# Linear attention and two feed-forward networks on one core: seven products reordered, one accumulation delayed, decode ticks and two attention steps changed

## Chip, core and metric

The kernel runs on one core of a Trainium2 chip. The metric is the device time of one execution in microseconds (us). The core's engines are TensorE (PE, with its weight loads listed as PEld), VectorE (DVE), ScalarE (ACT), GpSimd (POOL) and SyncE (SP), which here only issues transfers. Each engine works through its own queue in order.

## What is computed

Linear attention over 8 batches of 8 heads (576 positions of 64), then a feed-forward network with squared ReLU (512 to 2048 to 512) and a gated one with a norm ahead of it (512 to 1536 to 512), for 4608 tokens, all in float32.

```python
q_s = softmax(q, axis=-1);  k_s = softmax(k, axis=2)      # both with the maximum taken off first
kv = einsum('bhsd,bhse->bhde', k_s, v)
x = einsum('bhsd,bhde->bhse', q_s, kv)                    # heads joined: (4608, 512)
h = relu(x @ w_in);  x = (h * h) @ w_out                  # first network
xn = x / sqrt(mean(x * x) + 1e-6) * rms_g                 # second network
g = xn @ w_gate
out = (g * sigmoid(g) * (xn @ w_val)) @ w_out2
```

## The kernel before

**Precision.** TensorE multiplies in a rounded format. Each float32 operand is split into a high half (ScalarE copies it into that format) and a low half (VectorE or GpSimd subtracts); `split` (L76) does this for activations. A product takes three passes (`PASSES`, L21): high by high, high by low, low by high, in this order. Only the third needs the low half of the activations when these are the first operand, as in the accumulations.

**First network.** Nine blocks of 512 tokens run one after the other, with 16 units each (`units`, L823). A unit c first makes its hidden slice (`p1_A`, L593: 12 matmuls into a `ps_h` bank, of which there are two; then ReLU at L589, square at L590 and the split of `g` at L77 and L78). Its second-layer product (`p1_B`, L608: 12 matmuls into four `acc` banks) follows `LAG` = 2 units later: the list `pending` (L906 to L908) holds the units that wait for it. After unit 15 the four banks are copied to `e` tiles, two by ScalarE (L622) and two by VectorE (L620), and stored; the next block's first accumulation into a bank waits for its copy. Below, h(n) and o(n) are the first- and second-layer products of the n-th unit over all blocks, so h(32) opens the third block.

**Beside it.** The attention of the next block runs between the units at fixed offsets (`A_STEPS`, `todo`): the maximum of k over positions (`a_kmax`, L402), its transposes (`ps_kt`, `ps_kb`), exponentials, k times v (`ps_kv`, `kvf`, `kvd`), the transposes of q (`ps_q`, `qT`) and `ps_x`, which becomes the next block's input. `a_qn` (L490) divides q by its row sums, on GpSimd. In the first block all attention steps come at the start, in an order written out at L880.

**Decode.** The weights arrive as 64-bit floats. `tick` (L325) moves a job through load, word steps (GpSimd L216, ScalarE L224), three VectorE steps (L235, L243, L247), and the split (ScalarE L251, GpSimd L252), and the halves go back to memory, to be streamed later through a ring of seven `ws` tiles. `n_ticks` (L825) says how many ticks have been made by unit i: the first network's weights in the first block, the second's (36 jobs with 512 values per partition, in groups of six) from the third block on, one tick in two units. The recording layer sorts instructions by readiness and this program order, so where a step stands in its engine's queue is not only set by the tick; steps marked `held` keep their place.

**Second network.** Again nine blocks. Each has six groups n. A group makes two pairs of hidden slices by seven products of half size instead of eight (`STEPS`, L707; p2_A, L724): sums of the weight quarters (a11, s2, a12, s1, s3, s4, a22) times sums of the input quarters (b11, t2, ...), 12 matmuls each, into the banks x, y, v and w. x takes a11 and a12, y takes s2 and s3, v takes s1 and s4. Between two products that share a bank, the first one's value is read out: `p1` (L769), `u2` (L771), `p5` (L776). The second-layer accumulations `p2_B` (L795) of the group before stand after the third and the fifth product. The weights stream in the order `order2` (L118 to L126), of which 16 keys are kept resident. `B_TASKS` (L843) make the next block's input meanwhile: load, squares (`sq`, L637, in `e` tiles, whose four buffers the output copies use too), norm, and the sums and splits of the input quarters.

Of the kernel before, what the change touches and what calls it, by code (L numbers as in the profile page):

```python
# [8 lines left out]
F32 = mybir.dt.float32  # L9
# [5 lines left out]
ALU = mybir.AluOpType  # L15
AX = mybir.AxisListType
# [8 lines left out]
def attention_moe_kernel(  # L25
# [12 lines left out]
    nc = tc.nc  # L38
    B, H, S, D = q.shape
    NT, DM = out.shape  # L40
    P = 128
# [5 lines left out]
    FF1 = w_in.shape[0]  # L47
# [67 lines left out]

    PROD = ("a11", "s2", "a12", "s1", "s3", "s4", "a22")  # L118
    order2 = []
    for n in range(NQ):  # L120
        order2 += [(w, n) for w in PROD[:3]]
# [280 lines left out]
    def a_kmax(j, hp):  # L402
        if j >= B:
            return
        mk = pools["a"].tile([P, 2, D], F32, tag="mk", name="mk", bufs=2)
        kt = kts[j, hp]
        m2 = pools["a"].tile([P, 2, 2, D], F32, tag="m2", name="m2", bufs=1)
        nc.vector.tensor_max(out=m2, in0=kt[:, :, 0:2, :], in1=kt[:, :, 2:4, :])
        nc.vector.tensor_max(out=mk, in0=m2[:, :, 0], in1=m2[:, :, 1])
        nc.vector.tensor_max(out=mk[0:SR], in0=mk[0:SR], in1=kt[0:SR, :, SF, :])  # L410
        mks[j, hp] = mk

# [77 lines left out]
    def a_qn(j, hp):  # L490
        qt = qts.pop((j, hp))
        rs = qms.pop((j, hp)).rearrange("p (h c) -> p h c", h=2).unsqueeze(3)
        qn = pools["a"].tile([P, NG, 2, D], F32, tag="qn", name="qn", bufs=2)
        ins = nc.gpsimd.tensor_tensor(
            out=qn.rearrange("p c h d -> p h c d"),
            in0=qt,
            in1=rs.to_broadcast([P, 2, NG, D]),
            op=ALU.mult,
        )
        held(j, ins)  # L500
        qns[j, hp] = qn
# [198 lines left out]
    def b_x(j, n):  # L700
# [6 lines left out]
    STEPS = (  # L707
        ("a11", "b11", "x"),
        ("s2", "t2", "y"),
        ("a12", "b21", "x"),  # L710
        ("s1", "t1", "v"),
        ("s3", "t3", "y"),
        ("s4", "b22", "v"),
        ("a22", "t4", "w"),
# [9 lines left out]
    def p2_A(j, n, step):  # L724
        a, b, bank = STEPS[step]
        w, x = wt[a, n], xos[j, b]
        if bank not in ps2:
            pool, tag = (ps_h, "h") if bank in "xy" else (ps_a, "a")
            ps2[bank] = pool.tile([P, 512], F32, tag=tag, name=f"ps_{bank}")
            first = True  # L730
        else:
            first = False
        ps = ps2[bank]
        last = bank == "w" or not first
        for g in range(2):
            for kk in range(2):
                for m, (wa, xa) in enumerate(PASSES):
                    nc.tensor.matmul(  # L738
                        ps[:, g * HF : (g + 1) * HF],
                        w[:, wa, (2 * g + kk) * P : (2 * g + kk + 1) * P],  # L740
                        x[:, xa, kk, :],
                        start=first and g == 0 and kk == 0 and m == 0,
                        stop=last and kk == 1 and m == 2,
                        skip_group_check=True,
                    )
        used((a, n), j)

        def sv(name):
            sv2[name] = pools["x"].tile([P, 512], F32, tag=name, name=name, bufs=1)
            return sv2[name]  # L750

        def add(name, in0, in1):
            nc.vector.tensor_tensor(out=sv(name), in0=in0, in1=in1, op=ALU.add)  # L753

        def r_tile(c):
            r = gp.tile([P, T], F32, tag="r", name="r", bufs=2)
            rs[c] = r
            return r

        def done(c):  # L760
            g = gp.tile([P, 2, T], F32R, tag="g", name="g")
            split(g, rs.pop(c))
            ghl[2, j, c] = g

        def two(t):
            return t.rearrange("p (one g f) -> p one g f", one=1, g=2)

        if step == 0:
            nc.scalar.activation(out=sv("p1"), in_=ps, func=AF.Copy)  # L769
        elif step == 1:  # L770
            add("u2", ps, sv2["p1"])  # L771
        elif step == 2:
            r = r_tile(2 * n)
            gate(1, two(ps2.pop("x")), r[:, 0:HF].unsqueeze(1))
        elif step == 3:
            nc.scalar.activation(out=sv("p5"), in_=ps, func=AF.Copy)  # L776
        elif step == 4:
            add("u3", ps2.pop("y"), sv2["p1"])
        elif step == 5:
            add("c12", ps2.pop("v"), sv2["u2"])  # L780
            gate(1, two(sv2["c12"]), rs[2 * n][:, HF:T].unsqueeze(1))
            done(2 * n)
        else:
            c2 = pools["x"].tile([P, 2, 2, HF], F32, tag="c2", name="c2", bufs=1)
            for t, in0, in1 in ((1, sv2["p5"], sv2["u3"]), (0, ps2.pop("w"), sv2["u3"])):
                nc.vector.tensor_tensor(
                    out=c2[:, t].rearrange("p g f -> p (g f)"), in0=in0, in1=in1, op=ALU.add
                )
            r = r_tile(2 * n + 1)
            gate(2, c2, r.rearrange("p (t f) -> p t f", t=2))  # L790
            done(2 * n + 1)
# [33 lines left out]
    def n_ticks(i):  # L825
        if i < FF1:
            return min(NJ1 + 3, 4 + sum(d <= i for d in due.values()))
        return min(NJ1 + 4 + max(0, i - 2 * FF1 - 1) // 2, len(jobs) + 4)


    A_STEPS = ((-3, a_loadk), (-2, a_loadq), (0, a_qmax), (0, a_kmax), (1, a_qsub), (1, a_ktr))
# [17 lines left out]
    with ExitStack() as ctx_a:  # L849
# [44 lines left out]
        for i, (j, c) in enumerate(units):  # L894
            if i == AHEAD:
                ctx_s.close()
                pools["r"] = ctx_r.enter_context(
                    tc.tile_pool(name="rp", bufs=1, reuse_waits="tile")
                )
            if i == 2 * FF1:  # L900
                ctx_r.close()
                pools["q"] = ctx_q.enter_context(
                    tc.tile_pool(name="qp", bufs=1, reuse_waits="tile")
                )
            p1_A(j, c)
            pending.append((j, c, None))  # L906
            if len(pending) > LAG:
                p1_B(*pending.pop(0)[:2])  # L908
            while ticks[0] < n_ticks(i):
                tick()  # L910
            if i > 2 * FF1 and outs:
                outs.pop(0)()
            if ticks[0] > NJ1 + 4:
                flush()
            for n, ja, hp, f in todo.get(i, ()):
                f(ja, hp)
            if i == n1 - FF1 - 1:
                assert not outs and ticks[0] == len(jobs) + 4
                flush(all=True)
                ctx_q.close()  # L920
                ctx_a.close()
                pools["x"] = ctx.enter_context(
                    tc.tile_pool(name="bp", bufs=1, reuse_waits="tile")
                )
                for key in res2[:NX]:
                    place(key)
            s = (i - (n1 - FF1)) * 3 - 6
            for at, f, args in B_TASKS:
                if s <= at < s + 3:
                    f(0, *args)  # L930
# [62 lines left out]
```

## Time and profile before

| | us |
|---|---|
| median of three runs (lowest, highest) | 1847.7 (1846.8, 1851.98) |
| the profiled execution's own time | 1849.58 |
| its span, first to last instruction | 1847.8 |
| TensorE busy in the span (share) | 1761.0 (95%) |
| VectorE busy | 1050.1 (57%) |
| ScalarE busy | 752.9 (41%) |
| GpSimd busy | 358.1 (19%) |
| mean granted TensorE clock | 0.981 |

A row of the timeline has start, duration, engine, line, operation, tiles (out<-in) and, in brackets, how long the engine stood before it and what ended that. [...] The first network's blocks end near 970 us, the second's fill the rest.

### The profile page before, as it was taken

What the parts mean: (1) busy time and instruction counts of PE and PEld (TensorE: products, weight loads), DVE (VectorE), ACT (ScalarE), POOL (GpSimd) and SP (SyncE); (2) the same over time, 40 slices, a digit from 0 to 9 for tenths busy, and PEclk for the clock granted to TensorE, in tenths of its full rate; (3) what the DMA queues carried; (4) which work ended last, traced back from release to release, by engine and by line L of the source; (5) the groups of instructions that cost most, each with busy time, mean ns of one, the idle gap of its engine ahead of it and who ended that gap; (6) DMA issues with size and microseconds to landing.
All of it is one profiled execution on the core that took longest, in us unless ns stands there. A gap on an engine that the chain in (4) does not pass through costs nothing.

```text
span 1847.8 us, 27313 instructions
## 1 busy us (share of the span) xinstructions
PE 1761.0 (95%) x10346; PEld 1526.1 (83%) x10346; DVE 1050.1 (57%) x1820; ACT 752.9 (41%) x1371; POOL 358.1 (19%) x353
## 2 busy tenths in 40 slices
PE   5789997998999899999999999999999999999998
PEld 3568886876887688788888989999999999998997
DVE  7876467366436633422245756576767675757544
ACT  4455444454445544443444232333333333333322
POOL 4666226145326612220000000000000000000000
PEclk8799998999999999999999999999999999999999
DMA  6677657578769866565757766767676767676673
GB/s 173 215 258 268 211 188 247 181 266 284 254 189 323 272 190 200 191 234 182 289 193 241 227 240 213 252 209 258 209 260 209 257 208 258 207 251 217 218 230 124
DMA packets 173634, 420.19 MB, mean 227 GB/s; under 512 B 57408, under 2 KB 74816, under 8 KB 172352
## 3 DMA queue, kind: packets, MB, share of 16 engines
q1 hardware_dynamic: 162272, 377.55, 62.6%
q10 hardware_dynamic: 11232, 40.90, 5.7%
q8 instruction: 83, 1.36, 0.3%
q14 instruction: 47, 0.39, 0.1%
HBM read 358.62 MB, written 59.77 MB: 226 GB/s over the span
## 4 chain that ended last, share of the span: by engine, by line
PE 68%; DMA 8%; DVE 3%; ACT 2%; POOL 1%; issue 1%; SPq 0%; POOLq 0%; ACTq 0%; DVEq 0%
PE acc L98 27%; PE ps_h L98 12%; PE ps_x L738 8%; PE ps_y L738 8%; PE ps_v L738 8%; PE ps_w L738 4%; DMA wd_a<-so 2%; DMA out<-e 2%; DMA wd_s<-so 2%; DMA qt<-in_q 1%; DMA wd_u<-so 1%; PE ps_x L98 1%; PE ps_kv L526 1%; DVE t L243 1%; DVE t L235 1%
## 5 line engine op out<-in xcount | busy, mean ns | idle before, releaser
L78 DVE TENSOR_TENSOR g<-r,g 128x512 fp32r<-128x512 f32 x252 | 191.2, 759 | 266.7 <-ACT g L77 264.5
L98 PE MATMUL acc<-g,ws 128*128 128x512 f32 x1296 | 317.0, 393 | 19.1 <-DVE e L620 8.1
L98 PE MATMUL ps_h<-x,ws 128*128 128x512 f32 x1296 | 329.5, 404 | 5.7 <-POOL ws L252 3.8
L98 PEld LDWEIGHTS acc<-g,ws 128*128 128x128 f32 x1296 | 243.9, 189 | 73.8 <-POOL ws L252 8.6
L98 PEld LDWEIGHTS ps_h<-x,ws 128*128 128x128 f32 x1296 | 245.2, 194 | 58.5 <-POOL ws L252 5.2
L98 PE MATMUL acc<-ws,g 128*128 128x512 f32 x1080 | 268.7, 394 | 0.0
L98 PEld LDWEIGHTS acc<-ws,g 128*128 128x128 f32 x1080 | 196.8, 190 | 36.8
L77 ACT ACTIVATE g<-r 128x512 fp32r<-128x512 f32 x252 | 157.6, 626 | 44.7 <-DVE r L722 30.9
L589 ACT ACTIVATE r<-ps_h 128x512 f32<-128x512 f32 x144 | 85.4, 593 | 194.8 <-PE ps_h L98 194.5
L720 ACT ACTIVATE sg<-c 128x256 f32<-128x256 f32 x108 | 56.5, 524 | 263.3 <-DVE c L753 213.3
L753 DVE TENSOR_TENSOR u<-ps_y,p 128x512 f32<-128x512 f32 x108 | 73.7, 682 | 125.9 <-PE ps_y L738 125.9
L738 PE MATMUL ps_x<-x,ws 128*128 128x256 f32 x972 | 130.7, 284 | 9.8 <-ACT p L769 9.8
L738 PEld LDWEIGHTS ps_x<-x,ws 128*128 128x128 f32 x972 | 122.2, 192 | 11.5 <-ACT p L769 11.4
L738 PEld LDWEIGHTS ps_v<-x,ws 128*128 128x128 f32 x864 | 114.2, 191 | 6.3
L738 PE MATMUL ps_v<-x,ws 128*128 128x256 f32 x864 | 116.0, 282 | 0.0
L98 PE MATMUL ps_h<-x,w 128*128 128x512 f32 x432 | 108.9, 399 | 0.0
L98 PE MATMUL acc<-g,w 128*128 128x512 f32 x432 | 106.9, 396 | 1.8 <-POOL w L252 1.4
L776 ACT ACTIVATE p<-ps_v 128x512 f32<-128x512 f32 x54 | 32.3, 597 | 176.5 <-PE ps_v L738 176.5
L738 PE MATMUL ps_y<-x,ws 128*128 128x256 f32 x756 | 101.0, 283 | 0.0
L98 PEld LDWEIGHTS acc<-g,w 128*128 128x128 f32 x432 | 82.3, 192 | 19.7 <-POOL w L252 1.9
L738 PEld LDWEIGHTS ps_y<-x,ws 128*128 128x128 f32 x756 | 95.7, 192 | 0.7
L98 PEld LDWEIGHTS ps_h<-x,w 128*128 128x128 f32 x432 | 80.0, 190 | 17.8 <-DVE x L78 0.5
(114 smaller groups left out, 2517.6 us busy)
## 6 DMA issues: line engine op xcount, KB each, us to landing
ws<-wd_s SPq DMA_DIRECT2D x135, 512.0 KB, 4.3
ws<-wd_a SPq DMA_DIRECT2D x117, 512.0 KB, 4.5
ws<-wd_o SPq DMA_DIRECT2D x96, 512.0 KB, 4.2
ws<-wd_i SPq DMA_DIRECT2D x90, 512.0 KB, 4.2
ws<-wd_u SPq DMA_DIRECT2D x90, 512.0 KB, 4.2
raw<-in_w_out SPq DMA_DIRECT2D x28, 512.0 KB, 4.8
raw<-in_w_gv SPq DMA_DIRECT2D x24, 512.0 KB, 5.2
wd_s<-so ACTq DMA_DIRECT2D x24, 512.0 KB, 5.4
```

Of the source, the lines that this page charges most:

```text
L77: held(j, nc.scalar.activation(out=dst[:, 0], in_=src, func=AF.Copy))
L78: nc.vector.tensor_tensor(out=dst[:, 1], in0=src, in1=dst[:, 0].bitcast(F32), op=ALU.subtract)
L98: ins = nc.tensor.matmul(ps, lhsT(a), rhs(b), start=first and n == 0, stop=last and n == 2)
L235: nc.vector.tensor_scalar(out=t, in0=sb, scalar1=3, scalar2=0x7FFFFFFF, op0=ALU.logical_shift_left, op1=ALU.bitwise_and,)
L243: nc.vector.scalar_tensor_tensor(out=t, in0=sb, scalar=0x80000000, in1=t, op0=ALU.bitwise_and, op1=ALU.bitwise_or)
L526: ins = nc.tensor.matmul(ps[h * D : (h + 1) * D, 0 : D + 1], ke[0:m, c, h, :], vt[0:m, c, h, :], start=c == 0, stop=c == SF,)
L589: nc.scalar.activation(out=r, in_=ps, func=AF.Relu)
L720: nc.scalar.activation(out=r, in_=h[:, :, 0], func=AF.Sigmoid)
L738: nc.tensor.matmul(ps[:, g * HF : (g + 1) * HF], w[:, wa, (2 * g + kk) * P : (2 * g + kk + 1) * P], x[:, xa, kk, :], start=first and g == ...
L753: nc.vector.tensor_tensor(out=sv(name), in0=in0, in1=in1, op=ALU.add)
L776: nc.scalar.activation(out=sv("p5"), in_=ps, func=AF.Copy)
```

## The change

Five edits, in the order of the file:

- **Order of products.** s1 becomes the third of the seven, a12 the fourth, in `STEPS` and in the order in which the weights stream (`PROD`). The gate of bank x moves behind a12, the copy `p5` behind s1. The accumulations still stand after the third and the fifth product.
- **Maximum of k.** Two pairwise maxima over the four position groups become one reduction along a strided view.
- **q in the first block** is normalized on VectorE instead of GpSimd.
- **Ticks.** From the third block on, ticks are made only in units 2 to 12 of a block, seven in ten units.
- **Block starts of the first network.** At unit 2 of every block but the first no second-layer product is issued; at unit 3 two are.

```diff
-    PROD = ("a11", "s2", "a12", "s1", "s3", "s4", "a22")
+    PROD = ("a11", "s2", "s1", "a12", "s3", "s4", "a22")
...
-        m2 = pools["a"].tile([P, 2, 2, D], F32, tag="m2", name="m2", bufs=1)
-        nc.vector.tensor_max(out=m2, in0=kt[:, :, 0:2, :], in1=kt[:, :, 2:4, :])
-        nc.vector.tensor_max(out=mk, in0=m2[:, :, 0], in1=m2[:, :, 1])
+        nc.vector.tensor_reduce(
+            out=mk, in_=kt[:, :, 0:SF].rearrange("p h c d -> p h d c"), axis=AX.X, op=ALU.max
+        )
...
-        ins = nc.gpsimd.tensor_tensor(
+        ins = (nc.gpsimd if j > 0 else nc.vector).tensor_tensor(
...
         ("s2", "t2", "y"),
+        ("s1", "t1", "v"),
         ("a12", "b21", "x"),
-        ("s1", "t1", "v"),
...
-        return min(NJ1 + 4 + max(0, i - 2 * FF1 - 1) // 2, len(jobs) + 4)
+        at = [n for n in range(2 * FF1 + 1, i + 1) if 2 <= n % FF1 <= 12]
+        return min(NJ1 + 4 + len(at) * 7 // 10, len(jobs) + 4)
...
-            if len(pending) > LAG:
+
+            while len(pending) > (LAG + 1 if j > 0 and c == LAG else LAG):
                 p1_B(*pending.pop(0)[:2])
```

The order on TensorE in the second network, first block, second group of products. `ps_x` is a11, then a12; `ps_y` s2, then s3; `ps_v` s1; the `acc` rows are the accumulation of the block's first hidden slice. Before:

```order
L738 MATMUL ps_x<-x,ws 128x256 x12
L738 MATMUL ps_y<-x,w_8235 128x256 x12
L738 MATMUL ps_x<-x,ws 128x256 x12
L98 MATMUL acc_9111<-ws,g 128x512 x3
L98 MATMUL acc_9112<-ws,g 128x512 x3
L98 MATMUL acc_9113<-ws,g 128x512 x3
L98 MATMUL acc_9114<-ws,g 128x512 x3
L738 MATMUL ps_v<-x,w_8237 128x256 x12
L738 MATMUL ps_y<-x,ws 128x256 x12
```

The same place on TensorE with the change:

```order
L738 MATMUL ps_x<-x,ws 128x256 x12
L738 MATMUL ps_y<-x,w_8171 128x256 x12
L738 MATMUL ps_v<-x,ws 128x256 x12
L98 MATMUL acc_9045<-ws,g 128x512 x3
L98 MATMUL acc_9046<-ws,g 128x512 x3
L98 MATMUL acc_9047<-ws,g 128x512 x3
L98 MATMUL acc_9048<-ws,g 128x512 x3
L738 MATMUL ps_x<-x,w_8173 128x256 x12
L738 MATMUL ps_y<-x,ws 128x256 x12
```

s1 and a12 have changed places around the accumulation, and the resident weight (`w_`, not `ws`) is another one.

The order on TensorE at the start of the third block in the first network. The first `ps_h` row is h(34), the `acc` rows are o(32), the block's first accumulation. Before:

```order
L98 MATMUL ps_h<-x,ws 128x512 x12
L98 MATMUL acc_2744<-g,ws 128x512 x3
L98 MATMUL acc_2745<-g,ws 128x512 x3
L98 MATMUL acc_2746<-g,ws 128x512 x3
L98 MATMUL acc_2747<-g,ws 128x512 x3
L419 MATMUL ps_kt<-ident,mk 128x128
L98 MATMUL ps_h<-x,ws 128x512 x12
```

The same place on TensorE with the change:

```order
L98 MATMUL ps_h<-x,ws 128x512 x12
L419 MATMUL ps_kt<-ident,mk 128x128
L98 MATMUL ps_h<-x,ws 128x512 x12
L98 MATMUL acc_2752<-g,ws 128x512 x3
L98 MATMUL acc_2753<-g,ws 128x512 x3
L98 MATMUL acc_2754<-g,ws 128x512 x3
L98 MATMUL acc_2755<-g,ws 128x512 x3
```

h(35) and a transpose of k now stand ahead of o(32).

The order on VectorE at the same block start, from the split of g(32) on; L620 are the copies of the second and the fourth bank, L235, L243 and L247 the decode. Before:

```order
L78 TENSOR_TENSOR g<-r,g 128x512
L235 TENSOR_SCALAR t_3646<-s 128x512
L243 SCALAR_TENSOR_TENSOR t_3646<-s,t_3646 128x512
L247 ISA t_3646<-t_3646,n 128x1024
L235 TENSOR_SCALAR t_3770<-s 128x512
L243 SCALAR_TENSOR_TENSOR t_3770<-s,t_3770 128x512
L235 TENSOR_SCALAR t_3909<-s 128x512
L247 ISA t_3770<-t_3770,n 128x1024
L620 COPY e<-acc_2089 128x512
L243 SCALAR_TENSOR_TENSOR t_3909<-s,t_3909 128x512
L620 COPY e<-acc_2091 128x512
L485 TENSOR_REDUCE qs<-qt 128x8
```

The same place on VectorE with the change:

```order
L78 TENSOR_TENSOR g<-r,g 128x512
L235 TENSOR_SCALAR t_3665<-s 128x512
L243 SCALAR_TENSOR_TENSOR t_3665<-s,t_3665 128x512
L247 ISA t_3665<-t_3665,n 128x1024
L235 TENSOR_SCALAR t_3745<-s 128x512
L243 SCALAR_TENSOR_TENSOR t_3745<-s,t_3745 128x512
L235 TENSOR_SCALAR t_3882<-s 128x512
L620 COPY e<-acc_2111 128x512
L243 SCALAR_TENSOR_TENSOR t_3882<-s,t_3882 128x512
L235 TENSOR_SCALAR t_3956<-s 128x512
L620 COPY e<-acc_2113 128x512
L78 TENSOR_TENSOR g<-r,g 128x512
```

One decode step less stands ahead of the first copy, one more between the two, and the next `g` follows the second copy directly.

## Rows read from the trace of the kernel before

**Rows 1.** Stages: start:end, length, busy by engine, clock, DMA share, GB/s

```profile
0.00:150.00 150.00, 108.83 (x525) 79.92 (x526) 114.33 (x216) 73.81 (x142) 88.39 (x98) 0.87 0.67 210
277.00:297.00 20.00, 10.09 (x37) 7.51 (x36) 18.95 (x21) 8.68 (x16) 14.84 (x14) 0.74 0.55 184
400.00:465.00 65.00, 55.45 (x271) 43.74 (x270) 44.37 (x78) 32.78 (x67) 40.50 (x39) 0.95 0.89 298
575.00:635.00 60.00, 51.70 (x238) 41.46 (x237) 39.27 (x61) 33.91 (x65) 40.45 (x35) 0.95 0.88 310
```

**Rows 2.** Waits of TensorE: who waited for whom, us in total, times, longest

```profile
PE ps_x L738 <- ACT p L769: 9.8, 8, 2.2
```

**Rows 3.** Timeline around 1090 us, TensorE, ScalarE and VectorE, second network

```profile
1086.30 1.60 PE L738 MATMUL ps_x<-x,ws 128*128 128x256 f32 x12
1087.74 1.60 PE L738 MATMUL ps_y<-x,w 128*128 128x256 f32 x12
1087.86 0.63 ACT L637 ACTIVATE sq<-x 128x512 f32<-128x512 f32 x1 [4.31 <-DMA out<-e]
...
1090.43 0.61 ACT L77 ACTIVATE g<-r 128x512 fp32r<-128x512 f32 x1
...
1090.95 0.58 ACT L769 ACTIVATE p<-ps_x 128x512 f32<-128x512 f32 x1
1091.31 0.69 DVE L78 TENSOR_TENSOR g<-r,g 128x512 fp32r<-128x512 f32 x1
...
1091.58 1.90 PE L738 MATMUL ps_x<-x,ws 128*128 128x256 f32 x12 [2.23 <-ACT p L769]
...
1093.28 4.34 PE L98 MATMUL acc<-ws,g 128*128 128x512 f32 x12
```

**Rows 4.** Timeline of TensorE at two other places of the eight

```profile
995.08 1.70 PE L738 MATMUL ps_x<-x,ws 128*128 128x256 f32 x12 [1.55 <-ACT p L769]
...
1188.63 1.69 PE L738 MATMUL ps_x<-x,ws 128*128 128x256 f32 x12 [1.19 <-ACT p L769]
1190.16 2.91 PE L98 MATMUL acc<-ws,g 128*128 128x512 f32 x12
```

**Rows 5.** Timeline at the start of the third block, TensorE, ScalarE, VectorE

```profile
277.15 2.88 PE L98 MATMUL ps_h<-x,ws 128*128 128x512 f32 x12
280.74 0.58 ACT L589 ACTIVATE r<-ps_h 128x512 f32<-128x512 f32 x1
281.86 0.98 PE L98 MATMUL acc<-g,ws 128*128 128x512 f32 x3 [1.83 <-ACT e L622]
...
289.13 1.13 DVE L247 CUSTOM_DVE_ANT_0 t<-t,n 128x1024 uint16<-128x1024 uint16 x1
290.19 0.68 DVE L620 COPY e<-acc 128x512 f32<-128x512 f32 x1
290.92 3.84 PE L98 MATMUL acc<-g,ws 128*128 128x512 f32 x9 [8.08 <-DVE e L620]
291.39 0.68 DVE L620 COPY e<-acc 128x512 f32<-128x512 f32 x1
...
292.58 1.50 DVE L78 TENSOR_TENSOR g<-r,g 128x512 fp32r<-128x512 f32 x1
```

**Rows 6.** Timeline of TensorE, the first burst's two waits in the fourth block

```profile
405.48 0.63 PE L508 MATMUL ps_q<-ident,qn 128*128 128x128 f32 x4 [1.02 <-DVE kvf L546]
412.71 0.86 PE L98 MATMUL ps_x<-qT,kvd 128*128 128x256 f32 x5 [1.00 <-DVE qT L78]
```

**Rows 7.** Instructions by line: duration in ns, least/median/most; first, last start; form

```profile
L408 DVE TENSOR_TENSOR m<-kt x32: 408/426/1534, 3.5 to 741.0; 128x256 f32<-128x256 f32 x32
L409 DVE TENSOR_TENSOR mk<-m x32: 272/292/1784, 3.9 to 742.3; 128x128 f32<-128x128 f32 x32
L471 DVE TENSOR_REDUCE qm<-qt x36: 655/685/690, 5.1 to 813.6; 128x8 f32<-128x512 f32 x36
L494 POOL TENSOR_TENSOR qn<-qt,qs x36: 1037/1044/1598, 15.6 to 860.9; 128x512 f32<-128x512 f32 x36
```

More of the change, by code (lines that the diff above doesn't have):

```diff
@@ L771, in p2_A @@
             add("u2", ps, sv2["p1"])
-        elif step == 2:
+        elif step == 3:
             r = r_tile(2 * n)
             gate(1, two(ps2.pop("x")), r[:, 0:HF].unsqueeze(1))
-        elif step == 3:
+        elif step == 2:
             nc.scalar.activation(out=sv("p5"), in_=ps, func=AF.Copy)
```

## The prediction

> **What bounds the kernel now.** I read the engine shares first, then TensorE's idle time by stage, then the list of its waits, and last the timelines around the longest of them. TensorE is the bound: outside four stretches and a few short waits it never stands, so a change is worth only what it takes out of TensorE's own idle time and out of the stretches at the lower clock around it. The table by stage [rows 1] shows the four: 41.2 us of idle in the first 150 us (150 − 108.83), 9.9 us in the 20 us around 277 to 297, 9.6 us in 400 to 465 and 8.3 us in 575 to 635. There the granted clock is 0.87, 0.74, 0.95 and 0.95. The list of waits [rows 2] gives the largest one behind 970 us: 9.8 us in eight waits of `ps_x` for the copy `p`. Whatever goes from these places comes off the span, unless TensorE stops for something else soon after.
>
> **Seven products in another order (second FFN, 9 blocks).** [Rows 3] is one of the eight places, the second group of products of a block. a11 starts at 1086.30, s2 at 1087.74, and a12, which adds to the same bank, could start at 1089.18. ScalarE must first copy `p` out of that bank, but its queue was held 4.31 us by a square (`sq`) whose buffer waited for the output store `out<-e`. `p` ends at 1091.53 and TensorE stands 2.23 us. After the change s1 stands there, which writes another bank that is free, so TensorE works on to 1090.62. Behind it stands the first accumulation of the block, and that needs `g`: the high half from ScalarE (1090.43 + 0.61 = 1091.04), the low half from VectorE (1091.31 + 0.68 = 1091.99). Two of the first three products need only the high half. They start near 1091.09 (0.05 behind the release, as a12 started 0.05 behind `p`) and take 0.46; the third starts at 1092.04 instead of 1090.62 + 0.46 = 1091.08. So 0.96 us of the 2.23 stays: the wait moves from `p` to `g` and is 1.27 us shorter. The a12 behind it finds `p` long done. All eight places have this shape, and `g` ends 0.41 us behind the wait's end at each. The two longest of the eight are 2.23 and 1.55 [rows 3, 4]; they leave 0.96 and 0.28. The other six are 6.0 us together, 1.0 each (1.19 in the one shown), and leave nothing. Of 9.8 us 1.3 stay, with a little over: **−8.5**. At 1091 the lower clock follows: a12 and the accumulation take 1.90 and 4.34 there and 1.69 and 2.91 at the next place [rows 3, 4], 1.6 us more. After the 1.55 us at 995 a12 took 1.70, so a wait of that length costs no clock, and 0.96 is shorter, so I take this back too: **−1.6**. Sum −10.1. Bounds: if all twelve products wait for the low half, 0.97 per place is won, 2.7 stay and the clock loss too, −7.1; if nothing stays, −11.4. What is late next: the gate of `ps_x` now comes after the accumulation, but its bank is wanted again only after s3, one accumulation, s4 and a22, 7.0 us at the durations above, for a sigmoid and two VectorE steps. The copy `p5`, for which s4 waits, comes earlier. The weights are streamed in the new order, the same number of loads on SyncE; which keys stay resident changes, their number doesn't.
>
> **Second-layer products a unit later at block starts (first FFN).** Only one boundary is costly, from the second block to the third [rows 5]: TensorE stands 1.83 and 8.08 us because four `acc` banks have to be copied out and VectorE has decode steps queued ahead of its two copies. Now: h(34) ends at 280.03. h(35) can go once its bank's old value has been read by ScalarE (280.74 + 0.58), so from 281.4 to 284.2. The first bank is ready, 0.7 us. On VectorE one decode step less (1.13 us at 289.13) stands ahead of the first copy, which ends near 289.9 instead of 290.87, and another takes its place ahead of the second, which ends near 291.7 instead of 292.07. The last bank's products then end near 292.6. Before, TensorE had the same work and h(35), 2.75 us, done only at 294.76 + 2.75 = 297.5. That is −4.9. The products after these need the low half of the next `g`, which then ends near 293 (now 292.58 + 1.50 = 294.08), close to when they get there, and I give 0.6 back: **−4.3**. Bounds: the covered unit alone, −2.7; the wait wholly gone with its lower clock, −6.5. The delayed products hold four `g` buffers, as many as there are.
>
> **Prep decode mid-block.** This changes the order of the work of VectorE, ScalarE and GpSimd, not its amount. In the order of VectorE, jobs stand in bursts before and after: ten at the third block's start in both, then four bursts of six and two single ones. The bursts move (now: the end of the third block into the fourth, the fourth's end, and twice mid-fifth), so the text "only mid-block" isn't what the engines do. Before, the four bursts lie behind the idle times of 400 to 465 and 575 to 635 [rows 1]. With the clock (0.05 of 65 and of 60 us) these cost 9.6 + 3.3 and 8.3 + 3.0, together 24 us. Which attention step a burst meets decides its price: the first burst's two waits [rows 6] are 2.0, the second's are the rest of that stretch, 9.55 − 2.0 = 7.5. Four times the one or the other is 8 to 30 us of idle against 18 now, so −10 to +12; I take **0**, the two kinds in equal number.
>
> **Maxima of k in one step.** Out go, 32 times, a step of 0.43 and one of 0.29 us by the medians, but they reach 1.53 and 1.78; in comes one reduction over 512 values. The nearest row is the maximum of q over 512 values, 0.66 to 0.69 in all 36 [rows 7]. By the medians that is a draw (0.72 against 0.69); what is won is the long cases. VectorE leads TensorE only in bursts and at the start, so **−2** as an estimate: four such steps there, 0.5 each. [...] The new reduction reads with a stride of 64 values, which no row shows. The far bound is the longest that the pair itself took, 1.53 + 1.78 = 3.3: +2.6 each.
>
> **Normalizing q on VectorE in the first block.** It takes four GpSimd steps of 1.04 us [rows 7] off GpSimd's queue and puts four of about 0.69 on VectorE, ahead of the copy that the first k transposes need. By the order `qn` comes about 1 us earlier and the k chain up to 2 us later. **0**, from −3 to +4.
>
> **Sum.** −10.1 − 4.3 + 0 − 2 + 0 = −16.4 against the profiled execution's 1849.6 us (span 1847.8), so 1833.2; the median of the runs lies 1.9 below that execution: **about 1832**.
>
> **Rivals.** (1) The wait in the second FFN only changes its name: if `g` comes a further 1.3 us late, each place stands as long as before. For it: the root, a square behind an output store, isn't touched. Against: ScalarE's order around it is unchanged. 1832 + 10 = 1842. (2) The strided reduction is slow. For it: every value read lies 256 bytes from the last, which no VectorE row of this trace does; against it: nothing measured. At the far bound the four reductions ahead of the first transposes cost 4 × 2.6 = 10.4 us: 1842. [...] (3) Slower: the mid-block bursts, now up to four jobs within a unit, meet the chain from `kvf` over `qT` to `ps_x` each time. At the 12.9 us that all of 400 to 465 cost, four bursts cost 52 against 24: 1832 + 28 = 1860. It ends on the slow side of no change only if each costs over 11 us ((24 + 16 + 5.5) / 4). Against: that stretch held two bursts. (4) The bursts all cost as the cheap one, 8 of idle instead of 18 and less clock loss: 1820.
>
> **How the numbers follow.** Forecast 0.64, rival (1) 0.10, (2) 0.08, (3) 0.08, (4) 0.10. A measurement of this kernel can tell about 0.3%, 5.5 us, from no change: faster is below 1842.2, slower above 1853.2. Faster: 0.64 + 0.10 + half of (1) + 0.02 of a mild (3) = 0.81. Slower: 0.06, the rest of (3) without a part that ends between. The same: 0.13. The range goes from 1820, where (4) lies, to 1846, above (1) and (2).
>
> **What would show it.** Right: `ps_x` waits for `p` gone from the list and in their place two or three waits of `acc` for `g` below 1 us; clock 1.00 around 1090; about 5 us of idle left at the boundary near 282; reductions of 0.7 us at the k maxima. Wrong: waits of `acc` for `g` as long as the old ones; k maxima above 1 us; more than 20 us of TensorE idle between 297 and 800, waiting for `kvf`, `qT` or `mk`; more than 42 us of idle in the first 150.

## The result and the profile after

The changed kernel takes 1825.2 us (median of four runs, 1822.4 to 1828.6) against 1848.6 (1846.8 to 1852.0): ratio 0.9872, 95% interval 0.9849 to 0.9895, 23.4 us less. Four later runs beside other kernels gave 1828.5 and a ratio of 0.988 (0.986 to 0.990), 22.2 less. The forecast was 1832, 16.4 less.

The profiled execution took 1822.4 us, with a span of 1820.6. Busy time of each engine, with its share of the span and its instructions, from its page:

```profile
PE 1751.3 (96%) x10346; PEld 1520.1 (83%) x10346; DVE 1062.1 (58%) x1792; ACT 750.9 (41%) x1371; POOL 351.9 (19%) x349
```

The span is 27.2 us shorter, and of that TensorE's busy time gives 9.7 and its idle time 17.5. The matmuls are the same, so a busy time that shrinks means that they took less time each (0.1702 us of busy time each before, 0.1693 after); the mean granted clock rose with it, from 0.981 to 0.986. The same stages as in [rows 1], in wider windows (columns as there), of the changed kernel:

```profile
0.00:150.00 150.00, 108.28 (x541) 79.78 (x542) 115.53 (x213) 75.58 (x147) 86.33 (x96) 0.92 0.70 218
260.00:330.00 70.00, 63.86 (x314) 51.40 (x313) 52.47 (x74) 34.91 (x67) 41.42 (x38) 0.95 0.74 244
330.00:650.00 320.00, 305.16 (x1573) 247.88 (x1572) 186.37 (x307) 160.91 (x302) 154.16 (x145) 0.97 0.80 265
```

and the same windows of the kernel before:

```profile
260.00:330.00 70.00, 60.09 (x297) 48.39 (x296) 55.28 (x75) 31.55 (x60) 41.63 (x38) 0.93 0.69 231
330.00:650.00 320.00, 302.01 (x1540) 244.40 (x1539) 170.09 (x306) 157.72 (x297) 144.42 (x138) 0.98 0.76 254
```

Window less TensorE's busy time is its idle time: 9.9 us before and 6.1 after at the third block's start, 18.0 and 14.8 from 330 to 650. In the first 150 us idle time is as in [rows 1] (41.7 and 41.2 us) and the granted clock rose from 0.87 to 0.92.

To compare stretches of kernels I add to the idle time what matmuls took beyond the usual, at the lower clock or for another reason (the granted clock in the traces before and after is 1.0 or 0.5 at any moment, 0.50 from 1094 to 1096 in the one before; a stretch has the mean): for each matmul the time to the start of the next, less idle time and less the median for its line and shape, summed over the stretch. The sum of both is called **lost time** below (the "slow matmuls" of the expectations are its second part). The first stretch counts from TensorE's first matmul, 4.7 to 5.2 us into the span. The k times v matmuls come about 7 or about 50 ns apart, so their median rests on a jump; taken as the mean of its two middle values instead of the upper one, the lost time of 330 to 650 is 2 to 6 us higher.

| lost time, us | 0–150 | 260–330 | 330–650 | 965–1790 |
|---|---|---|---|---|
| before | 62.6 | 12.7 | 30.2 | 16.7 |
| changed, first profile | 57.1 | 9.3 | 23.9 | 4.3 |
| changed, second profile | 58.0 | 10.0 | 31.5 | 4.2 |

The second row's 23.9 is not a property of the kernel: the second profile of the same program has 31.5 there. So the profile's 27.2 us flatters the change, and terms below are judged by medians where there are any.

TensorE's longest waits after (total, times, longest; compare [rows 2]):

```profile
PE ps_kt L419 <- DVE mk L410: 13.9, 5, 5.1
PE ps_x L98 <- DVE qT L78: 7.3, 5, 2.9
...
PE acc L98 <- DVE e L620: 5.6, 1, 5.6
...
PE ps_kv L526 <- issue: 5.3, 1, 5.3
...
PE acc L98 <- DVE g L78: 0.7, 3, 0.3
```

`ps_x` no longer waits for `p`; what is left of those 9.8 us are two of the three waits of `acc` for `g`, 0.2 us each (the third lies in the first network).

### The profile page after: what moved, and what is told of

Its sections match the earlier page's. It is cut to its first block, busy times and chain, and to the rows that moved or that the text cites. A ratio compares the mean times of both kernels' runs of the same rounds, so it can differ in the third digit from the quotient of the medians.

```text
span 1820.6 us, 27274 instructions
## 1 busy us (share of the span) xinstructions
PE 1751.3 (96%) x10346; PEld 1520.1 (83%) x10346; DVE 1062.1 (58%) x1792; ACT 750.9 (41%) x1371; POOL 351.9 (19%) x349
## 4 chain that ended last, share of the span: by engine, by line
PE 75%; DMA 4%; DVE 2%; POOL 2%; issue 1%; ACT 1%; POOLq 0%; ACTq 0%; SPq 0%; DVEq 0%
PE acc L98 30%; PE ps_h L98 14%; PE ps_y L738 8%; PE ps_x L738 8%; PE ps_v L738 8%; PE ps_w L738 4%; DMA wd_s<-so 1%; DMA wd_a<-so 1%; POOL so L252 1%; PE ps_x L98 1%; PE ps_kv L526 1%; DMA wd_u<-so 1%; DVE t L243 1%; DVE t L235 0%; PE ps_q L508 0%
## 5 line engine op out<-in xcount | busy, mean ns | idle before, releaser
L98 PE MATMUL ps_h<-x,ws 128*128 128x512 f32 x1296 | 325.0, 401 | 6.7 <-POOL ws L252 5.9
L98 PEld LDWEIGHTS ps_h<-x,ws 128*128 128x128 f32 x1296 | 242.4, 192 | 59.3 <-POOL ws L252 7.9
L720 ACT ACTIVATE sg<-c 128x256 f32<-128x256 f32 x108 | 56.5, 524 | 273.0 <-DVE c L753 223.0
L753 DVE TENSOR_TENSOR c<-ps_v,u 128x512 f32<-128x512 f32 x54 | 37.4, 692 | 105.1 <-PE ps_v L738 105.1
L98 PEld LDWEIGHTS ps_h<-x,w 128*128 128x128 f32 x432 | 81.7, 194 | 17.5
L590 ACT ACTIVATE r<-r 128x512 f32<-128x512 f32 x144 | 89.9, 628 | 3.0
```

Of the source, the lines that this page charges most:

```text
L98: ins = nc.tensor.matmul(ps, lhsT(a), rhs(b), start=first and n == 0, stop=last and n == 2)
L590: nc.scalar.activation(out=r, in_=r, func=AF.Square)
L720: nc.scalar.activation(out=r, in_=h[:, :, 0], func=AF.Sigmoid)
```

## The experiments: one part at a time

Four kernels have one edit of the change each, on top of the kernel before; two are the changed kernel with one edit put back; one has the new reduction with its stride taken away. Each ran beside the kernel before, and what it wins is worked out from the ratio of the two. For the first four the kernel before has a median of 1847.3 us over 27 runs; by the medians alone they win 9.8, 3.9, 1.8 and 1.4 us.

**Order of products alone.**

```diff
-    PROD = ("a11", "s2", "a12", "s1", "s3", "s4", "a22")
+    PROD = ("a11", "s2", "s1", "a12", "s3", "s4", "a22")
...
         ("s2", "t2", "y"),
+        ("s1", "t1", "v"),
         ("a12", "b21", "x"),
-        ("s1", "t1", "v"),
...
```

The gate of bank x and the copy `p5` change places with them, as in the whole change.

> The kernel before with the new order of the seven products alone. By the prediction's term (8.5 us of waits and 1.6 us of clock) the time falls by 10.1 us, from 1848.6 to about 1838. The rival takes the whole difference of the two traces behind 965 us (idle time and slow matmuls together, 20.7 us before against 6.7 after): a fall of 14, to about 1834.5; then this term was too small by 4. If the waits only changed their name, about 1848.

1837.5 us, ratio 0.9946 (0.9933 to 0.9960): 10.0 us less, from 7.4 to 12.4. That is the prediction's term; the rival's 14 lies outside. In the profile the lost time of 965 to 1790 falls from 16.7 to 4.5, which is 9.3 us of idle time and 2.9 of faster matmuls. The place of [rows 3] in this kernel, timeline with start, duration, engine, line, operation, tiles and the idle time before it:

```profile
1084.50 1.60 PE L738 MATMUL ps_x<-x,ws 128*128 128x256 f32 x12
1085.37 0.63 ACT L637 ACTIVATE sq<-x 128x512 f32<-128x512 f32 x1 [3.62 <-DMA out<-e]
1085.94 1.60 PE L738 MATMUL ps_y<-x,w 128*128 128x256 f32 x12
...
1087.38 1.60 PE L738 MATMUL ps_v<-x,ws 128*128 128x256 f32 x12
...
1087.93 0.62 ACT L77 ACTIVATE g<-r 128x512 fp32r<-128x512 f32 x1
...
1088.82 0.68 DVE L78 TENSOR_TENSOR g<-r,g 128x512 fp32r<-128x512 f32 x1
1088.82 3.33 PE L98 MATMUL acc<-ws,g 128*128 128x512 f32 x12
```

ScalarE's square still stands 3.62 us for the output store, as it stood 4.31 before; TensorE doesn't notice. The accumulation starts right behind s1, and its third pass finds the low half (1088.82 + 0.68 = 1089.50) with 0.10 us to wait, not the 0.96 forecast: the square ended 1.50 us behind a11's start (1085.37 + 0.63 − 1084.50), not 2.19 as in [rows 3], so `g` came that much earlier. The accumulation takes 3.33 us instead of 4.34; the granted clock is 1.00 from 1084 to 1093, where it was 0.67 from 1093 to 1098 before.

**Block starts alone.**

```diff
-            if len(pending) > LAG:
+            while len(pending) > (LAG + 1 if j > 0 and c == LAG else LAG):
                 p1_B(*pending.pop(0)[:2])
```

> The kernel before with the later second-layer product at the block starts alone. By the prediction's term a fall of 4.3 us, to about 1844, with some 5 us of TensorE's idle time left near 286. By the two traces (12.7 us of idle and slow matmuls in 260 to 330 against 9.3) a fall of 3.4. The rival is that the decode that follows undoes it: about 1848, with the wait of acc for the copy e as long as before.

1843.5 us, ratio 0.9985 (0.9974 to 0.9997): 2.8 us less, from 0.6 to 4.8. The wait of `acc` for `e` is 5.9 us instead of 8.1, and the lost time of 260 to 330 is 11.1 instead of 12.7. Smaller than the term of 4.3, which the interval still holds.

**Decode ticks alone.**

```diff
-        return min(NJ1 + 4 + max(0, i - 2 * FF1 - 1) // 2, len(jobs) + 4)
+        at = [n for n in range(2 * FF1 + 1, i + 1) if 2 <= n % FF1 <= 12]
+        return min(NJ1 + 4 + len(at) * 7 // 10, len(jobs) + 4)
```

> The kernel before with the moved decode ticks alone. By the prediction nothing, about 1848.6, since cheap and costly bursts cancel. The rival is that the ticks bring what the traces differ by in 330 to 965 us (33.9 us of idle and slow matmuls before against 24.3 after): a fall of 9.5, to about 1839, with TensorE's idle time in 400 to 650 below 15 us instead of 18. The other rival is the reverse, a rise of up to 12.

1845.5 us, ratio 0.9984 (0.9974 to 0.9995): 3.0 us less, from 0.9 to 4.8. Neither of the rivals; the term of nothing lies just outside. From 330 to 965 the lost time falls from 33.9 to 28.0: the waits of the old places (405 to 461, 581 to 630) are gone, and new ones stand at 391 (1.1 us), 472 (3.0), 517, 529 (3.8), 558 and 567 to 570.

The longest of the old waits from 400 to 465, in the kernel before, with the last decode step on VectorE ahead of it and the first one behind:

```profile
414.75 0.64 DVE L247 CUSTOM_DVE_ANT_0 t<-t,n 128x1024 uint16<-128x1024 uint16 x1
...
424.10 0.69 DVE L471 TENSOR_REDUCE qm<-qt 128x8 f32<-128x512 f32 x1 [5.67 <-DMA qt<-in_q]
...
427.73 0.35 DVE L546 SCALAR_TENSOR_TENSOR kvf<-ps_kv,rk,mask 128x128 f32<-128x128 f32 x1
...
428.23 0.63 PE L508 MATMUL ps_q<-ident,qn 128*128 128x128 f32 x4 [2.45 <-DVE kvf L546]
...
439.40 0.43 DVE L235 TENSOR_SCALAR t<-s 128x512 uint32<-128x512 uint32 x1 [3.40 <-POOL so L252]
```

VectorE makes no decode step for 24 us here. The product that `kvf` reads was done at 420.04 (`ps_kv`, 419.09 + 0.95), but the maxima of q and of k stand ahead of it on VectorE, which stood 5.67 us for the load of q. This wait and the 0.59 us at 435 are 3.0 of the 7.5 us that the prediction put down to the second burst.

**One reduction for the maximum of k alone.**

```diff
-        m2 = pools["a"].tile([P, 2, 2, D], F32, tag="m2", name="m2", bufs=1)
-        nc.vector.tensor_max(out=m2, in0=kt[:, :, 0:2, :], in1=kt[:, :, 2:4, :])
-        nc.vector.tensor_max(out=mk, in0=m2[:, :, 0], in1=m2[:, :, 1])
+        nc.vector.tensor_reduce(
+            out=mk, in_=kt[:, :, 0:SF].rearrange("p h c d -> p h d c"), axis=AX.X, op=ALU.max
+        )
```

> The kernel before with the maximum of k in one reduction alone. By the prediction a fall of 2 us, to about 1846.5. The first rival takes the difference of the traces in the first 150 us (62.6 us of idle and slow matmuls before, 57.1 after) as the reduction's work: a fall of 5.5, to about 1843. The second takes the reduction's 1.07 us against the 0.72 us of the pair's medians: four of them at the start cost 1.4 us more, about 1850.

1845.9 us, ratio 0.9985 (0.9972 to 0.9998): 2.8 us less, from 0.4 to 5.2, as forecast and with 1.07 us for each reduction. The lost time of the first 150 us is 60.8 instead of 62.6. The first four pairs took 4.9 us together and the first four reductions 4.1; the first ten took 13.1 and 10.5.

**The pair of maxima put back** in the changed kernel:

```diff
-        nc.vector.tensor_reduce(
-            out=mk, in_=kt[:, :, 0:SF].rearrange("p h c d -> p h d c"), axis=AX.X, op=ALU.max
-        )
+        m2 = pools["a"].tile([P, 2, 2, D], F32, tag="m2", name="m2", bufs=1)
+        nc.vector.tensor_max(out=m2, in0=kt[:, :, 0:2, :], in1=kt[:, :, 2:4, :])
+        nc.vector.tensor_max(out=mk, in0=m2[:, :, 0], in1=m2[:, :, 1])
```

> The changed kernel with the two pairwise maxima of k put back. From the one reduction alone (a fall of 2.8, interval 0.4 to 5.2) the time rises by 2 to 3 us against the changed kernel's 1825.2, to about 1828. The rival: the reduction's 1.07 us against the pair's 0.72 us makes it the worse form once the startup has changed too, about 1824, or nothing to see within 2 us.

1830.5 us, ratio 0.9908 (0.9889 to 0.9926), against 0.9872 and 0.988 with the reduction. The sign is the expected one. The size, 5 to 7 us by these ratios and 2 to 5 by the medians, is not, but each ratio is known to some 3.5 us on either side, which doesn't tell 3 from 7.

**q of the first block back on GpSimd**, likewise:

```diff
-        ins = (nc.gpsimd if j > 0 else nc.vector).tensor_tensor(
+        ins = nc.gpsimd.tensor_tensor(
```

> The changed kernel with q of the first block normalized on GpSimd again. The four edits tried alone sum to 10.0 + 2.8 + 3.0 + 2.8 = 18.6 us; the whole change gave 23.4. If VectorE's four steps are the rest, this rises by about 5, to 1830, and the waits of ps_q for the GpSimd tile qn (3.3 us in each run with the old form) come back. By the prediction's term of 0 it stays at 1825.

1828.7 us, ratio 0.9908 (0.9891 to 0.9925): slower than the changed kernel by 5 to 7 us by ratios, by 0.2 and 3.5 by the medians of its two sets. The wait of `ps_q` for `qn` did not come back; `ps_q` waits 2.3 us for the sums `qs` instead. The lost time of the first 150 us is steadier than the total. By what a kernel has of these two edits:

| lost time, 0–150 us | least to most | mean | profiles |
|---|---|---|---|
| pair, qn on GpSimd | 61.3 to 62.7 | 62.3 | 4 |
| reduction, qn on GpSimd | 60.8 to 60.9 | 60.9 | 2 |
| pair, qn on VectorE | 59.3 | 59.3 | 1 |
| reduction, qn on VectorE | 56.5 to 59.6 | 58.1 | 7 |

(One of the seven has the reduction of the next experiment.) So the step on VectorE is worth some 3 us of lost time at the start and the reduction 1.2 to 1.4; the total times can't tell either from the spread between sets, as the last run below shows.

**The same reduction without the stride**, in the changed kernel. It takes four neighbours instead of four values 256 bytes apart.

```diff
-            out=mk, in_=kt[:, :, 0:SF].rearrange("p h c d -> p h d c"), axis=AX.X, op=ALU.max
+            out=mk, in_=kt[:, :, 0:SF].rearrange("p h c (d f) -> p h (c d) f", f=4), axis=AX.X, op=ALU.max
```

> The changed kernel with the reduction over four values that lie side by side instead of 256 bytes apart; instruction, sizes and results per partition are the same, but each of the 128 results is the maximum of other values (the softmax does not depend on which number is taken off). If the stride makes 1.07 us out of the 0.69 of the reduction over 512 values in L471, the line falls to about 0.69; the time to about 1824, four times 0.4 us at the start. The rival: 128 results of four values cost 1.07 us whatever the stride, and the time stays at 1825.

The line's durations (least/median/most in ns; first and last start; form), first of the changed kernel:

```profile
L407 DVE TENSOR_REDUCE mk<-kt x32: 1017/1074/1105, 3.6 to 724.7; 128x128 f32<-128x512 f32 x32
```

and with neighbours:

```profile
L407 DVE TENSOR_REDUCE mk<-kt x32: 667/685/687, 3.5 to 728.4; 128x128 f32<-128x512 f32 x32
```

The stride alone makes 1.07 us out of 0.69. The time stays, 1825.1 us and ratio 0.9884 (0.9863 to 0.9904): the 1.6 us that four reductions at the start could give are too few to be seen in an interval of 3.8 us on either side.

## The experiments: what the bursts are

The moved ticks left bursts, and TensorE still loses 33 us and more between 260 and 650. The start of the third block in the changed kernel, TensorE and VectorE:

```profile
279.69 0.84 PE L98 MATMUL acc<-g,ws 128*128 128x512 f32 x3
280.14 2.67 DVE L243 SCALAR_TENSOR_TENSOR t<-s,t 128x512 uint32<-128x512 uint32 x1
282.95 0.69 DVE L247 CUSTOM_DVE_ANT_0 t<-t,n 128x1024 uint16<-128x1024 uint16 x1
283.56 0.88 DVE L235 TENSOR_SCALAR t<-s 128x512 uint32<-128x512 uint32 x1
284.47 0.69 DVE L243 SCALAR_TENSOR_TENSOR t<-s,t 128x512 uint32<-128x512 uint32 x1
285.08 0.42 DVE L235 TENSOR_SCALAR t<-s 128x512 uint32<-128x512 uint32 x1
285.41 0.68 DVE L620 COPY e<-acc 128x512 f32<-128x512 f32 x1
...
286.15 4.27 PE L98 MATMUL acc<-g,ws 128*128 128x512 f32 x9 [5.62 <-DVE e L620]
```

Five decode steps stand ahead of the first copy on VectorE; that is TensorE's 5.62 us. TensorE's longest wait from 330 to 650 has such steps behind it, too:

```profile
513.56 1.64 DVE L243 SCALAR_TENSOR_TENSOR t<-s,t 128x512 uint32<-128x512 uint32 x1
...
516.80 1.75 DVE L247 CUSTOM_DVE_ANT_0 t<-t,n 128x1024 uint16<-128x1024 uint16 x1
518.46 0.28 DVE L421 TENSOR_REDUCE mc<-ps_kt 128x1 f32<-128x128 f32 x1
518.84 1.55 PE L526 MATMUL ps_kv<-vt,ke 128*64 128x65 f32 x20 [5.31 <-issue]
```

The view names no releaser. But the attention's products share two banks, and TensorE starts 0.10 us behind the end of `mc`, which reads `ps_kt`; in the second profile (5.85 us) and in the kernel with the moved ticks alone (3.83 us) it starts the same 0.10 us behind `mc`.

**Decode kept in place.** The first VectorE step of each of the 36 jobs is marked `held`, so that it stays where the ticks put it.

```diff
-        nc.vector.tensor_scalar(
+        hold = 0 if key[0] in ("i", "o") else 1
+        ins = nc.vector.tensor_scalar(
             out=t,
             in0=sb,
             scalar1=3,
...
+        held(hold, ins)
```

> The changed kernel with the first VectorE step of each job of the second network's weights kept at its place in program order, so that in VectorE's order the 36 jobs stand one in a unit through units 3 to 13 of five blocks, instead of ten at the third block's start and four bursts of six. If the bursts make TensorE's idle time there (6.1 us in 260 to 330 and 14.8 in 330 to 650, with 3.1 and 9.0 of slow matmuls), most goes: a fall of some 20 to 28 us against the changed kernel, to about 1800, and no wait of acc for e above 2 us. The rival: what makes the waits is the amount of VectorE's work, and a single job in a unit delays the chain from kvf to ps_x as well: 36 waits of about 0.5 us, time about 1820 to 1830.

1819.1 us, ratio 0.9859 (0.9834 to 0.9883). The boundary is clean: the lost time of 260 to 330 falls from 9.3 to 0.4, and no wait of `acc` for `e` is left. But 330 to 650 keeps 25.2, so the expected 20 to 28 us did not come: the wait for `mc` is gone, and others have come in its place. An even decode on VectorE is not enough there. The longest wait left, TensorE and ScalarE with its stores (ACTq), of this kernel (its L253 is L251, L436 is L434):

```profile
532.17 0.63 ACT L253 ACTIVATE so<-t 128x512 fp32r<-128x512 f32 x1 [1.00 <-DMA wd_s<-so]
532.24 0.34 ACTq L266 DMA_DIRECT2D wd_a<-so  x1
...
535.23 2.88 PE L98 MATMUL acc<-g,w 128*128 128x512 f32 x12
...
540.51 0.63 ACT L253 ACTIVATE so<-t 128x512 fp32r<-128x512 f32 x1 [5.52 <-DMA wd_a<-so]
...
541.05 0.26 ACT L436 ACTIVATE mb<-ps_kb 128x128 f32<-128x128 f32 x1
...
541.45 0.85 PE L510 MATMUL ps_q<-ident,qn 128*128 128x128 f32 x4 [3.34 <-ACT mb L436]
```

ScalarE stands 5.52 us at a split of a weight sum into a `so` tile (there are four): its buffer waits for a store that was issued 8.3 us before. `mb`, which TensorE wants, is queued behind. ScalarE's waits for `so` buffers, in total, times, longest, were there in the kernel before:

```profile
ACT so L251 <- DMA wd_s<-so: 27.0, 12, 4.7
ACT so L251 <- DMA wd_a<-so: 23.4, 11, 4.5
ACT so L251 <- DMA wd_u<-so: 4.9, 4, 1.8
```

55.3 us, which the prediction did not read; 16.3 of them lie between 400 and 465. With the old ticks these waits are 43 to 56 us (four kernels), with the moved ones and the decode free 36 to 46 (six profiles).

**Stores a unit earlier**, on top of the held decode:

```diff
             w_split(t, f(), nc.gpsimd)
-            send(key, t, 2)
+            send(key, t, 1)
```

> The kernel with the held decode (1819.1), with the stores of the sums' halves issued one unit after the split instead of two. In it ScalarE stands 30.4 us in 12 waits of so for the store wd_a<-so, up to 5.5, and TensorE's longest wait left (3.3 us at 541 for mb) lies behind one. If these waits make what is left in 330 to 650 (12.7 us idle, 12.5 of slow matmuls), an earlier store takes a good part of it: about 1808 to 1813. The rival: the store is late because the transfers of that stretch are slow, and an earlier issue moves the waits elsewhere: 1819 within 3 us.

1825.6 us, ratio 0.9873 (0.9852 to 0.9894): no gain, but 6.5 us more by the medians and 2.6 by the ratios. The lost time of 330 to 650 is 35.5. At one of its waits:

```profile
569.43 1.26 POOL L254 TENSOR_TENSOR so<-t,so 128x512 fp32r<-128x512 f32 x1
...
570.73 0.33 ACTq L266 DMA_DIRECT2D wd_a<-so  x1
571.10 0.63 ACT L77 ACTIVATE g<-r 128x512 fp32r<-128x512 f32 x1 [3.10 <-POOL so L254]
571.63 0.58 ACT L77 ACTIVATE qT<-ps_q 128x512 fp32r<-128x512 f32 x1
...
572.27 0.63 PE L98 MATMUL ps_x<-qT,kvd 128*128 128x320 f32 x1 [3.60 <-ACT qT L77]
```

The earlier store now waits on ScalarE's queue until GpSimd's half of `so` is made (569.43 + 1.26 = 570.69), and `g` and `qT` wait behind it. The rival held: the wait moved.

**The splits kept in place too.** Against the kernel with the held decode:

```diff
-            w_split(t, f(), nc.gpsimd)
-            send(key, t, 2)
+            held(1, nc.scalar.activation(out=t[:, 0], in_=f(), func=AF.Copy))
+            nc.gpsimd.tensor_tensor(
+                out=t[:, 1], in0=f(), in1=t[:, 0].bitcast(F32), op=ALU.subtract
+            )
+            send(key, t, 1)
...
-            d_out(key, lambda: floats.pop(key))
+            d_out(key, lambda: floats[key])
```

> The same with the ScalarE half of each sum's split also kept at its place in program order, so that these splits no longer stand in groups of two to four ahead of the attention's copies. If ScalarE's waits for the so buffers are the second cause of the idle time in 330 to 650, they fall below 5 us in all and the time comes to about 1800 to 1808. The rival: the splits' fixed places make GpSimd and the stores later instead, and TensorE's waits only change their names: 1815 to 1822.

1795.5 us, ratio 0.9703 (0.9682 to 0.9724), faster than either kernel, and 30.0 us below the kernel without this last edit. Now no wait of `so` for a store is left, and ScalarE's waits for GpSimd's half of `so` are 5.3 us in three. The traces show why. Without this edit a split ran as soon as a buffer was free (22 of 50 started within 0.2 us of the landing of the store four splits before), while its own store kept its place and came 17.4 us later by the median; the buffer was held all that time. With the edit the store follows 5.7 us behind the split, and no split comes within 0.2 us of that landing. The groups of the expectation don't explain it by themselves: splits back to back are as common in the next kernel, which has no such wait either. The windows of this kernel:

```profile
260.00:330.00 70.00, 70.00 (x369) 57.18 (x369) 34.67 (x66) 32.02 (x60) 20.36 (x23) 1.00 0.64 199
330.00:650.00 320.00, 318.29 (x1664) 260.57 (x1663) 173.94 (x310) 166.26 (x311) 145.69 (x139) 0.99 0.82 270
```

1.7 us of idle time in 330 to 650 instead of 22.0 without this edit and 14.8 in the changed kernel, at a DMA share no lower than before (0.76 and 0.80): the transfers were not the limit, the order on the engines was.

**The splits kept in place, the decode free**, the fourth corner: the last diff alone on the changed kernel.

> The changed kernel with the ScalarE half of each sum's split kept in place and its store a unit earlier, but with VectorE's decode free to stand in bursts. With the held decode (9.3 us of idle and slow matmuls in 260 to 330 gone, 330 to 650 at 25 as before) and with both (330 to 650 at 4.5) this is the fourth corner. If the splits' bursts on ScalarE alone make the waits of 330 to 650, those go here too and the boundary's 9 us stay: about 1805. The rival: there VectorE's bursts and ScalarE's waits each suffice, so that only both edits together take them out: 1815 to 1825, with waits of ps_x for the VectorE half of qT as before.

1811.1 us, ratio 0.9801 (0.9788 to 0.9814), between the two theories. Side by side:

| | us | lost 260–330 | lost 330–650 |
|---|---|---|---|
| changed kernel, two profiles | 1825.2, 1828.5 | 9.3, 10.0 | 23.9, 31.5 |
| decode held | 1819.1 | 0.4 | 25.2 |
| decode held, stores earlier | 1825.6 | 0.9 | 35.5 |
| splits held, stores earlier | 1811.1 | 8.2 | 15.8 |
| both held, stores earlier | 1795.5 | 0.3 | 4.5 |

The third block's start belongs to VectorE's decode: 8.2 of the 9 to 10 us stay with the splits held, and next to nothing without the bursts. From 330 to 650 the early splits on ScalarE are the larger cause, but with them gone the bursts on VectorE still cost 11 us by lost time, or 8 to 10 by the total times (15.6 by the medians and 18.1 by the ratios, less 7.9 at the third block's start), and with them present the even decode gains nothing there. No kernel holds the splits with the stores at their old place, so what the earlier store does by itself then is not shown.

**The changed kernel once more**, beside the two of the same set:

> The changed kernel once more, beside the two below: 1825, from 1822 to 1829, and idle times of TensorE between 330 and 650 us that sum to about 15. If the runs with one part put back (1828.7 and 1830.5) lie apart from it only by the spread of the runs, this gives 1828 or more.

1828.5 us, from 1825.8 to 1829.9, and 20.2 us of idle time from 330 to 650 where its first profile had 14.8. So up to some 3 us between a kernel and the changed one is spread between sets, and by the test of this expectation the total times of the runs with one part put back (1828.7 and 1830.5) tell little; what is said of those parts rests on the ratios and on the lost time.

## Why the prediction was right, and where it was not

The time fell inside the range and on the forecast's side, 4 to 7 us below the forecast itself.

- **Seven products, −10.1:** right in size (−10.0) and in mechanism. The wait moved from `p` to `g`. Both parts were put too low: 0.5 us of waits stayed in that kernel, not 1.3, since the square came earlier relative to the products than [rows 3] had it, and the faster matmuls gave 2.9 us, not 1.6. The lost time fell by 12.2 us and the run by 10.0; the interval holds both, so that the term was met to 0.1 us is in part luck.
- **Block starts, −4.3:** −2.8 alone, and in the changed kernel 3.4 us of lost time less at this place. The forecast said some 5 us of idle would stay; 5.6 did. What the term lacks is small, and the interval of 0.6 to 4.8 holds it; as far as one profile tells it lies in the decode steps around the copies, of which two took 2.67 and 1.77 us where it had counted 1.13 for one.
- **Decode ticks, 0:** the term that failed. It was −3.0, and the price it rested on was misread. It gave the first burst 2.0 us and the second the rest of 400 to 465, 7.5, by the releasers on VectorE. But 3.0 of the 7.5 came while VectorE made no decode step, behind a late load of q. With 4.5 in its place the same sum, two bursts of each kind, gives 13 us against 18, so −5 as an estimate, not 0. It also looked at one engine of two: in the changed kernel holding VectorE's decode left 330 to 650 as it was, holding ScalarE's splits (with their stores earlier) took 8 to 31 us of lost time out of it, and only both took nearly all. No run held either in the kernel before. Why the moved ticks won 3 us is open; that ScalarE's waits for `so` are fewer with them goes with it, but doesn't show it.
- **Maximum of k, −2:** right in size (−2.8, and 1.4 at the start), for a reason that was half wrong. The price of 0.69 us taken from [rows 7] was not met: the strided reduction takes 1.07. A reduction above 1 us was among the prediction's signs of being wrong, and it came; rival (2) had this right, but its far bound of 3.3 us was far from the truth. At 1.07 the four steps that the term counted save 0.8 us, not 2; ten at the start save 2.6. What carries the gain, as far as the durations tell, is what the term said would: the pair's long cases are gone, since 32 pairs that took 689 + 535 ns on average became 32 reductions between 1017 and 1105. In the kernel before, no step of the pair that ran without a GpSimd step beside it took more than 426 and 293 ns, and the long ones, up to 1534 and 1784 [rows 7], all ran beside one. In the changed kernel the 19 reductions that ran beside a GpSimd step took 1023 to 1105 ns, the 13 others 1017 to 1096. No run here took GpSimd's work away, so that it made the pair's steps long is not shown. The reduction's own price is the stride's, 1.07 us against 0.69 in the run with neighbours; why a stride costs that, no run shows.
- **q on VectorE, 0:** about −3 by the lost time of the start, at the edge of the bounds given; the total times don't show it. Most of what the forecast lacks is this and the ticks: −3 and −3.
- **Sum:** the four edits tried alone give 18.6 us, with some 3 for q 21.6, against 22.2 and 23.4 measured. The rest is within the intervals.
- **Rivals:** (1) fell: no wait came back under the name of `g`. (3) fell: the mid-block bursts cost no more than the old ones. (4) would have been 1820 by cheap bursts; they were not cheap (24 to 32 us of lost time stays), and the time came from elsewhere. (2) is answered above.

## What to carry to other kernels

When one engine waits for another in bursts, read the waits of the engine that is named, too: a copy that comes late may be queued behind a step that itself waits for a store, and only that engine's own list of waits (here 55 us of ScalarE for `so`) shows it. Work that a scheduler moves forward because its inputs are ready still takes a place in its engine's queue: with the held decode a split of a weight sum stood 5.52 us for its buffer, `mb` started behind it, and TensorE stood 3.34 us for `mb`. Steps off the critical path that wait for buffers are better pinned where their buffers are free, on all engines at once. Holding the decode alone won 2 to 9 us here, by ratios and medians, holding the splits alone (with earlier stores) 13 to 17, both 30 to 33. How long a step's buffer is held shows in the distance from the step to the store that frees it (17.4 us here by the median, 5.7 with both held). And judge a stretch by more than one profile: the same program lost 23.9 and 31.5 us in one.

## What the runs showed of the hardware

- VectorE's reduction of 512 float32 values per partition into 128 took 0.69 us over neighbours and 1.07 us over values 256 bytes apart (medians of 32 each); the same instruction with the same sizes otherwise.
- Where TensorE stood 0.1 us instead of 2.23 us ahead of it, the accumulation behind ran 12 matmuls in 3.33 us at a granted clock of 1.00 instead of 4.34 at 0.67; over the second network 9.3 us less idle time brought 2.9 us of faster matmuls with it.
- With the held decode, a store of 512 KB released its buffer 8.3 us after its issue (532.24 to 540.51, as the wait's releaser has it), against a median of 4.5 us for these stores over that kernel; k, v and weights were being loaded meanwhile.
- In the kernel before, the two steps of VectorE's pair of maxima took at most 426 and 293 ns where no GpSimd step ran beside them (13 and 17 cases), and up to 1534 and 1784 ns where one did (19 and 15 cases, short ones among them). The changed kernel's reduction took at most 1096 ns without and 1105 ns with one beside it (13 and 19 cases).
